# Linear attention and MoE kernel: chunks handled in pairs, two tokens per partition

## The chip, the cores and the metric

The kernel runs on one core of a Trainium2 chip. The metric is the device time of one execution in microseconds; the time of the kernel before is the median of the runs shown. TensorE (PE) multiplies matrices, VectorE (DVE), ScalarE (ACT) and GpSimd (POOL) work element by element, SyncE (SP) issues DMAs.

## The reference

For 4 batches and 8 heads of 768 tokens with 48 channels, a recurrent linear attention with a decay for each channel feeds a two-layer MoE:

```python
for t in range(S):                       # S = 768, D = 48
    state = alpha[:, :, t, :, None] * state + np.einsum('bhd,bhe->bhde', k[:, :, t], v[:, :, t])
    y[:, :, t] = np.einsum('bhd,bhde->bhe', q[:, :, t], state)
x = y.transpose(0, 2, 1, 3).reshape(B * S, H * D)       # 3072 x 384
h = x @ w_in                                            # w_in 384 x 2048
r = np.maximum(h, 0.0)
g = s * (r * r) + b
return (g @ w_out).astype(np.float32)                   # w_out 2048 x 384
```

## The kernel before

The tokens are cut into 24 blocks of 128 (six per batch), one token on each partition. The recurrence is worked out by blocks. A block's logarithms of alpha (L292, ScalarE) are summed down the tokens by a matmul with a triangle of ones (L298), and four tiny matmuls give the sum over the whole block (L303). ScalarE takes exp of the sums and of their negatives (L312, L315) and of the last sums (L316). VectorE multiplies q by the first and k by the second (L325, L330). q and k are then transposed, in the first nine blocks by TensorE (L342) with a copy out of PSUM by VectorE (L365), and after those by a DMA transpose that ScalarE's queue issues (L347). A matmul makes k times v for the state (KV, L356), with v cast to bf16 on GpSimd (L319). VectorE adds the old state (L381, or L377 at the start of a batch) and GpSimd scales it by the block's decay (L392). TensorE makes the 128 by 128 scores of all heads (A, L398), VectorE masks them (L407), 28 small matmuls make y (L436), and ScalarE copies y into the MoE's input (L460).

The MoE works on groups of blocks, four groups of two blocks and four of four. Its first layer (L482) is 48 matmuls of 256 or 512 columns per group, read out by ScalarE's Relu (L491) and squared on VectorE (L499). Its second layer (L506) is 16 matmuls of 384 columns for each block, scaled and shifted by VectorE (L517) and stored from SP's queue (L529). The b part of g is carried by column sums of w_out (L264, L269) and a matmul at L279. w_in and w_out arrive in four quarters each through four staging tiles (`wst`), are cast by ScalarE (L243, L256), and are loaded between the first blocks.

PSUM holds `ct_ps` (sums, then transposes), `a_ps` (scores), `py_ps` (KV, then y), two tiles for the first layer and two for the second.

The order of all instructions is fixed ahead of time by a planner, the class `Schedule`. Each operation is recorded with an engine, a planned length, a priority, and the buffers that it reads and writes. The planner plays the engines forward and emits the instructions in the order of planned starts. The order on an engine's queue therefore doesn't change at run time; an instruction that waits holds those behind it. `want(n)` sets the due time of a block's attention, `NPE` the number of blocks transposed on TensorE, and from block `NAY` on, the scores of a block are issued in one piece with y of the block before. `LOADS` gives the order of the first loads on SP's queue. In gaps that the planner foresees before the second layer starts, `fill` issues matmuls without use (L674).

Of the kernel before, what the change touches and what calls it, by code (L numbers as in the profile page):

```python
# [21 lines left out]
NPE = 9  # L22

NAY = 13
# [5 lines left out]
LOADS = ["b0", "b1", "i0", "b2", "b3", "i1", "i2", "i3", "b4", "o0", "b5", "o1", "o2", "b6", "o3"]  # L30
# [100 lines left out]
def kernel(  # L131
# [16 lines left out]
    C = 128  # L148
    NCH = S // C
    NP = H // 2  # L150
    NBLK = B * NCH
    d_model = moe_w_in.shape[0]
    d_ff = moe_w_in.shape[1]
    NJ = d_ff // 128
    NIN = 5
# [5 lines left out]
    ct_ps = ps.tile([128, 512], FP32, name="ct_ps")  # L161
    cum_ps = ct_ps[:, 0:384].rearrange("a (h d) -> a h d", h=H)
    bl_ps = ct_ps[:, 384 : 384 + NP]
    t_ps = ct_ps.bitcast(BF16).rearrange("a (x p t) -> a x p t", x=2, p=NP)
    a_ps = ps.tile([128, 2, NP, 128], FP32, name="a_ps")
    py_ps = ps.tile([128, 512], FP32, name="py_ps")
    p_ps = py_ps[:, 0:384].rearrange("a (p e) -> a p e", p=NP)
    y_ps = py_ps[:, 0:384].rearrange("a (k t) -> a k t", k=3)
# [3 lines left out]
    def many(name, n, shape, dtype, zero=None):  # L172
        tiles = []
        for i in range(n):
            t = sb.tile(shape, dtype, name=f"{name}{i}")
            if zero is not None:
                zero.memset(t, 0.0)
            tiles.append(t)
        return tiles


    a_in = many("a_in", NIN, [128, H, D], FP32)
    q_in = many("q_in", NIN, [128, H, D], FP32)
    k_in = many("k_in", NIN, [128, H, D], FP32)
    v_in = many("v_in", NIN, [128, H, D], FP32)
# [3 lines left out]
    def load(n, src, dst):  # L189
        b, c = n // NCH, n % NCH  # L190
        nc.sync.dma_start(  # L191
            out=dst[n % NIN],
            in_=src[b, :, c * C : (c + 1) * C, :].rearrange("h s d -> s h d"),
# [4 lines left out]
    nc.scalar.preload_act_table_set("natural_log_exp_and_others")  # L198

    la_sb = many("la", 2, [128, H, 64], BF16, zero=nc.vector)  # L200
    U_bf = sb.tile([128, 128], BF16, name="U_bf")
    make_upper_triangular(nc, U_bf, 1.0, diag=True)
    ident_bf = sb.tile([128, 128], BF16, name="ident_bf")
# [3 lines left out]
    ones_col_bf = sb.tile([128, 1], BF16, name="ones_col_bf")  # L207
    nc.vector.memset(ones_col_bf, 1.0)
    vp_sb = many("vp", 4, [128, NP, VW], BF16, zero=nc.gpsimd)
    mask = sb.tile([128, 128], BF16, name="mask")  # L210
    make_upper_triangular(nc, mask, 1.0, diag=True)
    b_sb = many("b_s", 2, [128, H, D], FP32)
    binv_sb = many("binv", 2, [128, H, D], FP32)
    qk_sb = many("qk", 3, [128, 2, H, 64], BF16, zero=nc.vector)
    qkT_sb = many("qkT", 3, [128, 2, NP, 128], BF16)
    am_sb = many("am", 2, [128, 2, NP, 128], BF16)
    blast_sb = many("blast", 2, [128, NP], BF16)
# [72 lines left out]

    def st_ln(n):
# [417 lines left out]
```

## Time and profile before

| what | value |
|---|---|
| median of 2 runs | 201.03 us (200.18 and 201.87) |
| span of the profiled execution, first to last instruction | 196.9 us |
| the profiled execution's own time | not given apart; the two runs lie 3.3 and 5.0 us above its span |
| busy: TensorE, VectorE, ScalarE, GpSimd | 176.7, 141.0, 109.1, 37.5 us |
| granted TensorE clock | 1.000 |
| DMA packets under 512 bytes | 116,256 of 122,936 |
| q, k, v and alpha load, one block and one tensor | 192 KB, 1,024 rows of 192 bytes |
| last quarter of w_out lands | 51.9 us |

Times in the profile count from the first instruction of the execution. Busy time of TensorE includes the matmuls without use. A line such as `L482` is the line in the kernel that issued the instruction; `SPq` and `ACTq` are the queues of those engines with the DMAs that they issue. In the chain of waits each step is followed back to what released it.

### The profile page before, as it was taken

To read this page: it belongs to the slowest core of one execution; us is meant where nothing else is said; L and a number is where in the kernel's file an instruction comes from. 1 tells how busy PE (TensorE), PEld (TensorE's weight loads), DVE (VectorE), ACT (ScalarE), POOL (GpSimd) and SP (SyncE) were. 2 spreads that over 40 slices of the span, in tenths; PEclk is the share of its full clock that TensorE was granted. 3 is DMA by queue.
4 is the path that set the end of the run, shared out by engine and by line. 5 is a ranking of instruction groups with operands and counts; after the bars stand their busy time and mean duration, and the time that the engine had idled before them with its cause. 6 is when DMAs were issued, how large, how long until landed. Compare 5 with 4: busy or idle time off the path is not lost.

```text
span 196.9 us, 4940 instructions
## 1 busy us (share of the span) xinstructions
PE 176.7 (90%) x1903; PEld 105.5 (54%) x1921; DVE 141.0 (72%) x288; ACT 109.1 (55%) x225; POOL 37.5 (19%) x63
## 2 busy tenths in 40 slices
PE   1789969658699999999999999999999999999992
PEld 1345557446365777766555555555555555555560
DVE  4357948679899879985999887897988544444221
ACT  4245588749674477555487655766764564444200
POOL 8622202200412212121213331032131000000000
PEclk9999999999999999999999999999999999999999
DMA  6999898997989999999999999999925210011122
GB/s 134 181 279 203 276 315 210 195 342 163 267 168 220 218 229 184 269 191 221 149 255 222 183 248 213 226 168 238 197 67 71 68 42 7 35 40 40 43 82 80
DMA packets 122936, 34.15 MB, mean 173 GB/s; under 512 B 116256, under 2 KB 121376, under 8 KB 122912
## 3 DMA queue, kind: packets, MB, share of 16 engines
q1 hardware_dynamic: 107008, 29.89, 68.7%
q10 hardware_dynamic: 15840, 3.93, 15.0%
q8 instruction: 15, 0.25, 0.6%
q14 instruction: 9, 0.07, 0.1%
q0 software_dynamic: 64, 0.00, 0.0%
HBM read 25.17 MB, written 4.72 MB: 152 GB/s over the span
## 4 chain that ended last, share of the span: by engine, by line
PE 65%; DMA 15%; SPq 10%; ACT 3%; DVE 3%; issue 2%; ACTq 0%; DVEq 0%
PE o_ps_69 L506 15%; PE o_ps_68 L506 14%; PE h_ps_67 L482 12%; PE h_ps_66 L482 12%; SPq L191 9%; PE py_ps L436 4%; DMA wst_183<-in_moe_w_in_dram 3%; DMA wst_182<-in_moe_w_out_dram 3%; DMA wst_181<-in_moe_w_out_dram 3%; DMA wst_184<-in_moe_w_out_dram 3%; PE a_ps L398 3%; DMA q_in_77<-in_q_dram 2%; PE ct_ps L298 1%; ACT w_out_bf L256 1%; PE py_ps L356 1%
## 5 line engine op out<-in xcount | busy, mean ns | idle before, releaser
L482 PEld LDWEIGHTS <-w_in_bf 128*128 128x128 bf16 x384 | 35.3, 98 | 22.4 <-ACT w_in_bf L243 1.0
L491 ACT ACTIVATE r_158<-h_ps_66 128x512 bf16<-128x512 f32 x48 | 28.9, 602 | 26.8 <-PE h_ps_66 L482 11.2
L491 ACT ACTIVATE r_159<-h_ps_67 128x512 bf16<-128x512 f32 x48 | 28.9, 602 | 4.6 <-PE h_ps_67 L482 1.8
L482 PE MATMUL h_ps_67<-xd_156,w_in_bf 128*128 128x512 bf16 (+1 forms) x71 | 16.2, 343 | 0.1
L482 PE MATMUL h_ps_66<-xd_156,w_in_bf 128*128 128x512 bf16 (+1 forms) x67 | 15.8, 341 | 0.3
L407 DVE TENSOR_TENSOR am_141<-a_ps,mask 128x1024 bf16<-128x1024 f32 x12 | 14.6, 1221 | 0.6 <-PE a_ps L398 0.4
L407 DVE TENSOR_TENSOR am_142<-a_ps,mask 128x1024 bf16<-128x1024 f32 x12 | 14.7, 1223 | 0.2
L482 PE MATMUL h_ps_66<-xd_155,w_in_bf 128*128 128x256 bf16 (+1 forms) x70 | 13.0, 306 | 1.1 <-ACT w_in_bf L243 0.8
L482 PE MATMUL h_ps_67<-xd_155,w_in_bf 128*128 128x256 bf16 (+1 forms) x71 | 13.0, 307 | 0.1
L674 PE MATMUL o_ps_68<-zeros,ident_bf 128*128 128x512 bf16 x41 | 12.0, 412 | 0.2
L312 ACT ACTIVATE b_s_129<-ct_ps 128x384 f32<-128x384 f32 x12 | 5.9, 492 | 8.5 <-PE ct_ps L303 6.4
L482 PE MATMUL h_ps_67<-xd_157,w_in_bf 128*128 128x256 bf16 (+1 forms) x46 | 9.6, 323 | 0.4 <-ACT r_159 L491 0.2
L312 ACT ACTIVATE b_s_128<-ct_ps 128x384 f32<-128x384 f32 x12 | 5.9, 489 | 7.1 <-PE ct_ps L303 2.4
L482 PE MATMUL h_ps_66<-xd_157,w_in_bf 128*128 128x256 bf16 (+1 forms) x45 | 9.6, 323 | 0.2
L460 ACT ACTIVATE xd_156<-py_ps 128x384 bf16<-128x384 f32 x10 | 4.9, 494 | 6.8 <-PE py_ps L436 3.5
L298 PE MATMUL ct_ps<-la_97,U_bf 128*128 128x384 bf16 x12 | 4.1, 340 | 4.2 <-POOL mask masks.py:65 4.1
L392 POOL TENSOR_TENSOR s_st_149<-t_147,blast_144 128x384 bf16<-128x384 bf16 x4 | 3.6, 906 | 15.3 <-DVE t_147 L381 7.9
L674 PEld LDWEIGHTS <-ident_bf 128*128 128x128 bf16 x45 | 4.2, 103 | 4.4 <-issue 1.6
L392 POOL TENSOR_TENSOR s_st_151<-t_145,blast_143 128x384 bf16<-128x384 bf16 x4 | 3.6, 904 | 14.5 <-DVE t_145 L381 7.1
L460 ACT ACTIVATE xd_155<-py_ps 128x384 bf16<-128x384 f32 x8 | 3.9, 493 | 3.9 <-PE py_ps L436 2.8
L315 ACT ACTIVATE binv_131<-ct_ps 128x384 f32<-128x384 f32 x12 | 5.9, 496 | 0.0
L315 ACT ACTIVATE binv_130<-ct_ps 128x384 f32<-128x384 f32 x12 | 5.9, 490 | 0.0
(263 smaller groups left out, 438.3 us busy)
## 6 DMA issues: line engine op xcount, KB each, us to landing
out_dram<-o_sb_176 SPq DMA_DIRECT2D x8, 192.0 KB, 3.0
out_dram<-o_sb_177 SPq DMA_DIRECT2D x8, 192.0 KB, 2.5
out_dram<-o_sb_178 SPq DMA_DIRECT2D x8, 192.0 KB, 2.4
a_in_70<-in_alpha_dram SPq DMA_DIRECT2D x5, 192.0 KB, 4.1
q_in_75<-in_q_dram SPq DMA_DIRECT2D x5, 192.0 KB, 5.1
k_in_80<-in_k_dram SPq DMA_DIRECT2D x5, 192.0 KB, 4.6
v_in_85<-in_v_dram SPq DMA_DIRECT2D x5, 192.0 KB, 4.0
a_in_71<-in_alpha_dram SPq DMA_DIRECT2D x5, 192.0 KB, 5.3
```

Of the source, the lines that this page charges most:

```text
L191: nc.sync.dma_start(out=dst[n % NIN], in_=src[b, :, c * C : (c + 1) * C, :].rearrange("h s d -> s h d"),)
L298: nc.tensor.matmul(out=cum_ps, lhsT=U_bf, rhs=la[:, :, 0:D], start=True, stop=True)
L312: nc.scalar.activation(out=b_sb[n % 2], in_=cum_ps, func=AF.Exp)
L315: nc.scalar.activation(out=binv_sb[n % 2], in_=cum_ps, func=AF.Exp, scale=-1.0)
L392: nc.gpsimd.tensor_tensor(out=s_sb[n % 3], in0=t1_sb[n % 2], in1=bl, op=ALU.mult)
L407: nc.vector.tensor_tensor(out=am_sb[n % 2].rearrange("a e p t -> a (e p) t"), in0=a_ps.rearrange("a e p t -> a (e p) t"), in1=mask.unsquee ...
L436: nc.tensor.matmul(out=y_ps[32 * (x % 4) : 32 * (x % 4) + 32, x // 4, :], lhsT=(st[:, p, c0 : c0 + 32] if e is None else vp[:, p, c0 + 48 ...
L460: nc.scalar.activation(out=xd_sb[g % 3][:, :, t * C : (t + 1) * C], in_=y_ps, func=AF.Copy)
L482: nc.tensor.matmul(out=hp[:, i * n : (i + 1) * n], lhsT=w_in_bf[:, kk, 128 * j : 128 * (j + 1)], rhs=xd_sb[g % 3][:, kk, 0:n], start=(kk = ...
L491: nc.scalar.activation(out=r_sb[w % 2], in_=h_ps[w % 2], func=AF.Relu)
L506: nc.tensor.matmul(out=op[:, 0:d_model], lhsT=gt_sb[j][:, c0 : c0 + C], rhs=w_out_bf[:, j, :], start=(j == 0), stop=(j == NJ - 1),)
L674: nc.tensor.matmul(out=o_ps[0], lhsT=ident_bf, rhs=zeros, start=True, stop=True)
```

## The change

Two blocks of 128 tokens become a pair. Token 2p and token 2p+1 of the pair lie on partition p (slot j = 0 and 1), so that a load reads 384 bytes in a row instead of 192; there are 48 such loads of 384 KB where there were 96 of 192 KB. The first half of the partitions (c = 0) is the first chunk of the pair, the second half the second chunk. Three pairs of input tiles take the place of five single ones.

The decay sums run over partitions, at half the resolution in tokens: alpha of both slots is multiplied (`st_aa`), and one Ln, one triangle matmul and one pair of exps serve both. The missing slot is made up by multiplying q of slot 0 by 1/alpha of slot 1 (`st_r1`, `st_qr`) and k of slot 0 by alpha of slot 1 (`st_ka`). V is needed by chunk: half the rows are cast in place on GpSimd, half are moved between the partition halves by VectorE (`st_vmove`), and a second cast copy (`vc`) serves KV. KV becomes 16 matmuls over 64 partitions for a pair. The transposes work on 16 blocks for a pair, on TensorE for the first three pairs (with copies shared by ScalarE and VectorE) and then as two DMA transposes of 64 partitions, now on SP's queue. The tokens of a chunk stay in the order (slot, partition) up to the copy of y, which puts them back in order. PSUM is divided anew: transposes share `a_ps` with the scores; the decay sums, KV and y share two tiles `x_ps`. From pair 2 on, `AHEAD` records the front of the next pair ahead of the back of this one. The loads of `s` and `b` move from GpSimd's queue to ScalarE's. The planner's lengths and the order of the first loads are set for this.

```diff
-NPE = 9
-NAY = 13
+NPE = 3
+NAY = 6
+AHEAD = 2
-LOADS = ["b0", "b1", "i0", "b2", "b3", "i1", "i2", "i3", "b4", "o0", "b5", "o1", "o2", "b6", "o3"]
+LOADS = ["p0", "i0", "i1", "p1", "i2", "i3", "o0", "o1", "p2", "o2", "o3"]
...
-    ct_ps = ps.tile([128, 512], FP32, name="ct_ps")
...
+    t_ps = a_ps.rearrange("a e p t -> a (e p t)").bitcast(BF16).rearrange(
+        "a (x b t) -> a x b t", x=2, b=2 * NP
+    )
+    x_ps = [ps.tile([128, 512], FP32, name=f"x_ps{i}") for i in range(2)]
+    cum_ps = x_ps[0][:, 0:384].rearrange("a (h d) -> a h d", h=H)
+    p_ps = [x[:, 0:384].rearrange("a (p e) -> a p e", p=NP) for x in x_ps]
+    y_ps = [x[:, 0:384].rearrange("a (k t) -> a k t", k=3) for x in x_ps]
...
     def load(n, src, dst):
-        b, c = n // NCH, n % NCH
+        b, c = n // PSEQ, n % PSEQ
         nc.sync.dma_start(
-            out=dst[n % NIN],
-            in_=src[b, :, c * C : (c + 1) * C, :].rearrange("h s d -> s h d"),
+            out=dst[n % NIN].rearrange("a h j d -> a h (j d)"),
+            in_=src[b, :, c * 2 * C : (c + 1) * 2 * C, :].rearrange(
+                "h (s j) d -> s h (j d)", j=2
+            ),
         )
...
+    nc.scalar.dma_start(out=b_col, in_=moe_b.to_broadcast((128, 1)))
+    nc.scalar.dma_start(out=s_col, in_=moe_s.to_broadcast((128, 1)))
...
+    def vector_or_gpsimd(n):
+        return nc.vector if n == 0 else nc.gpsimd
+
+    def st_aa(n):
+        a = a_in[n % NIN]
+        vector_or_gpsimd(n).tensor_tensor(
+            out=aa_sb[0], in0=a[:, :, 0, :], in1=a[:, :, 1, :], op=ALU.mult
+        )
+
     def st_ln(n):
-        nc.scalar.activation(
-            out=la_sb[n % 2][:, :, 0:D], in_=a_in[n % NIN], func=AF.Ln
-        )
+        nc.scalar.activation(out=la_sb[n % 2][:, :, 0:D], in_=aa_sb[0], func=AF.Ln)
+
+    def st_r1(n):
+        nc.scalar.activation(out=r1_sb[0], in_=a_in[n % NIN][:, :, 1, :], func=AF.Ln)
+        nc.scalar.activation(out=r1_sb[0], in_=r1_sb[0], func=AF.Exp, scale=-1.0)
+
+    def st_qr(n):
+        x = q_in[n % NIN][:, :, 0, :]
+        nc.gpsimd.tensor_tensor(out=x, in0=x, in1=r1_sb[0], op=ALU.mult)
+
+    def st_ka(n):
+        x = k_in[n % NIN][:, :, 0, :]
+        vector_or_gpsimd(n).tensor_tensor(
+            out=x, in0=x, in1=a_in[n % NIN][:, :, 1, :], op=ALU.mult
+        )
...
     def st_vcast(n):
-        nc.gpsimd.tensor_copy(
-            out=vp_sb[n % 4].rearrange("a p (x d) -> a p x d", d=D)[:, :, 0:3:2, :],
-            in_=v_in[n % NIN].rearrange("a (p e) d -> a p e d", e=2),
-        )
+        for c in range(2):
+            nc.gpsimd.tensor_copy(
+                out=v_heads(vp_of(n, c), half(c)), in_=v_slot(n, c, c)
+            )
+            nc.gpsimd.tensor_copy(
+                out=vc_sb[n % 2][half(c)].rearrange("a (p e) d -> a p e d", e=2),
+                in_=v_slot(n, c, 1 - c),
+            )
+
+    def st_vmove(n):
+        for c in range(2):
+            nc.vector.tensor_copy(
+                out=v_heads(vp_of(n, c), half(1 - c)), in_=v_slot(n, c, 1 - c)
+            )
...
-        nc.scalar.dma_start_transpose(
-            out=qkT_sb[n % 3].rearrange("a x p t -> a (x p) t"),
-            in_=qk_sb[n % 3].rearrange("a x h d -> a (x h d)"),
+    def st_Tdma(n, c):
+        nc.sync.dma_start_transpose(
+            out=qkT_sb[n % 3][:, c].rearrange("a x p (j t) -> a (x p j) t", j=2),
+            in_=qk_sb[n % 3][half(c)].rearrange("a x p j e d -> a (x p j e d)"),
         )
...
     def st_KV(n):
         for p in range(NP):
-            nc.tensor.matmul(
-                out=p_ps[:, p, :],
-                lhsT=kb[:, 128 * p : 128 * p + 128],
-                rhs=vp[:, p, 0:3:2, :],
-                start=True,
-                stop=True,
-            )
+            for j in range(2):
+                for c in range(2):
+                    v = v_heads(vp_of(n, c), half(c)) if j == c else vc[half(c)]
+                    nc.tensor.matmul(
+                        out=p_ps[c][:, p, :],
+                        lhsT=kb[half(c), p, j, :],
+                        rhs=v[:, p],
+                        start=(j == 0),
+                        stop=(j == 1),
+                    )
...
+    for n in range(NPAIR):
+        while begun < min(NPAIR, n + (2 if n >= AHEAD else 1)):
+            add_pair(begun)
+            begun += 1
+        finish_pair(n)
```

## The prediction

> **What bounds the kernel now.** I read the page first, then the chain of waits in order of time, then a table of busy time by stretch, then single lines in the timeline.
>
> ```profile
> PE 176.7 (90%) x1903; PEld 105.5 (54%) x1921; DVE 141.0 (72%) x288; ACT 109.1 (55%) x225; POOL 37.5 (19%) x63
> PE   1789969658699999999999999999999999999992
> PE 65%; DMA 15%; SPq 10%; ACT 3%; DVE 3%; issue 2%; ACTq 0%; DVEq 0%
> ...
> 46.10 5.80 DMA wst_184<-in_moe_w_out_dram
> 51.92 1.49 ACT w_out_bf L256
> 53.45 0.81 PE o_ps_68 L506 x4
> ```
>
> The chain has two parts. Up to 53.45 us it runs over SP's queue and the DMA of weights: the last quarter of w_out lands at 51.92, is cast, and the matmul that needs it starts at 53.45. From there it is TensorE almost alone, to 193.05. So the end is 53.45 plus what TensorE still has to do, and what can be won lies in the 53.45 and in TensorE's own work.
>
> ```profile
> 15.00:19.00 4.00, 3.95 (x60) 2.13 (x59) 3.31 (x6) 2.16 (x7) 1.30 (x2) 1.00 1.04 205
> 33.00:35.00 2.00, 1.95 (x24) 1.66 (x23) 0.95 (x4) 0.55 (x2) 0.20 (x1) 1.00 1.09 365
> 90.00:140.00 50.00, 49.24 (x547) 27.15 (x555) 43.29 (x82) 32.85 (x78) 11.51 (x15) 1.00 1.24 214
> 150.00:190.00 40.00, 39.84 (x278) 21.71 (x280) 18.20 (x37) 16.39 (x28) 0.00 (x0) 1.00 0.19 52
> ```
>
> Columns: stretch, length, busy PE, PEld, DVE, ACT, POOL, granted clock, DMA share, GB/s. With the 192-byte loads alone the full DMA moves 205 GB/s, with weights alone 365. From 90 to 140 TensorE is full, and VectorE has only 6.7 us of 50 free; after 150 VectorE is under half busy.
>
> **TensorE's work, counted.** Up to 53.4 us the trace has 7 decay sums (L298 and L303, 0.27 from start to the next line's start), 7 transpose sets (0.45), 7 KV (0.25), 6 A (0.33), 6 y (0.5; the first 0.33), 102 first-layer matmuls of 256 columns (0.108 each, six in 0.65) and 12 second-layer ones (0.1625, four in 0.65): 1.9+3.2+1.8+2.0+2.8+11.0+2.0 = 24.7 us. So 28.7 of the first 53.45 us are idle or filler (L674). What follows is 139.6 us without a gap; total work 164.3.
>
> **The loads.** Ahead of the last weight quarter SP issues 7 blocks (5.50 MB) now, 3 pairs (4.72 MB) after. Now: 2.5 us until data flows, 5.50/0.205 = 26.8, weights 6.29/0.365 = 17.2, together 46.5; the trace says 51.9, so 5.4 go where SP waits for staging tiles. For 384-byte packets no row exists. Bounds: 205 GB/s (twice the bytes take twice the time) and 365 (the weights' rate). A fixed part and a part by bytes, drawn through 192 bytes at 205 (15.0 ns for a packet of one engine) and 2,048 bytes at 365 (89.8 ns), gives 22.7 ns, or 270 GB/s; I take it, being nearer the 192-byte row in size. Then 2.5+17.5+17.2+5.4 = 42.6 instead of 51.9 (at 205: 48.1; at 365: 38.0).
>
> The Trainium skill, "DMA: Bandwidth & Descriptors", Specifications, speaks against a large gain: it puts line rate at 512 bytes and up, with a read-modify-write below, and 384 is below. Read strictly, 384 bytes would stay at the 192-byte row's 205 GB/s and the sum would be 5.5 us worse; that page's section "Why small descriptors are slow (HBM only)" has a fixed cost per packet instead, which is on the side of the middle value. No row here decides.
>
> **What TensorE gets done before that moment.** The cast ends 1.5 later, at 44.1. By then pairs 0 and 1 are through (per pair: sum 0.27, two transpose sets 0.9, KV 0.66, two A 0.66, two y 1.0, first pair 0.83; 6.8 in all), pair 2 has its front and one A (1.5), groups 0 and 1 their first layer (96 x 0.108 = 10.4), the two open output tiles three quarters (24 x 0.1625 = 3.9), and the bias matmul (1.3): 23.9. Idle 44.1 - 23.9 = 20.2 instead of 28.7: **8.5 off** (3.0 to 13).
>
> One new wait takes some back. From pair 2 on, the next pair's front is recorded ahead of this pair's back, and the decay sum and KV share x_ps[0]. So KV of pair 2 stands behind the sum of pair 3, whose alpha is loaded after the last weights: 42.6 + 1.5 transfer + product 0.9 + Ln 0.5 + sum 0.3 + Exp 1.2 = 47.0; y of both chunks and their copies end near 51. The second layer of groups 0 and 1 covers it (64 x 0.1625 = 10.4, less the 3.9 done: until 50.6). I charge **+1.0** for joints; with that cover gone it is 7.
>
> **TensorE's own work after.** Sums: 12 fewer x 0.27 = -3.2. Transposes: 6 blocks instead of 9, -1.4. KV: 16 matmuls of 64 rows per pair; A's eight of 64 rows take 0.33, so 0.66 instead of 2 x 0.25, +1.9 over 12 pairs (bounds: no change, or 16 x 0.0625 = 1.0 per pair and +6). Sum **-2.7** (-4.6 to +1.4). A, y and the MoE are as before.
>
> **What moves to other engines.** Per pair:
> - ScalarE: one Ln, one pair of Exps and a copy of the last sums less (0.5+0.49+0.49+0.19), a Ln and an Exp more (1.0); two transpose issues leave its queue (1.25 each). It gets freer by 3.2 us; off the path.
> - SP: gets two transposes, 18 in all where ScalarE had 15, at 1.25 to 1.95 (L347's shortest and longest row) beside four loads at 1.5 (their transfer) and two stores at 0.36: 9 to 11 of 13 us. The DMA engines spent 15.0% of the span on 15 transposes, 2.0 us each; A pair then has 5.8 of loads, 4.0 of transposes and 1 of stores: 10.8 of 13. If blocks of 64 rows cost double it is 14.8; but the share of 1.24 above shows the two kinds overlapping in the engines, so I keep 10.8 and no charge, with (14.8 - 13.0) x 9 = +16 as the far bound. A transpose that waits for q and k holds the stores and loads behind it; the loads are three pairs ahead and there are three output tiles, which hide one such wait. Not hidden, the late store stops VectorE's L517, then L506.
> - The s and b loads leave POOL (0.74 + 0.54) for ScalarE's queue, and the b product no longer stands before the first V cast (which began at 10.13): about 2 us of the first chain, given to the added product, Exp and multiplies of pair 0. Zero.
> - VectorE: two half-partition V moves. Bounds 0.25 (a 256-column square is 0.28) and 0.55 (a q product); I take 0.3 each, 0.6. The two Tcopies after the sixth block were already gone from the ninth. A pair has 4 x 0.47 + 4 x 0.36 + 2 x 1.22 for q, k, state and mask, and for its share of the MoE 8 squares at 0.34 and 2 x 0.61: 9.7, which becomes 10.3, beside 13.0 on TensorE (10.4 MoE, 2.6 attention).
> - POOL: two casts and two state products (2.8) become four casts (4 x 0.5), three products (L392's 0.85 each) and two state products: 6.3.
> - The y of an odd chunk from the eleventh on is recorded after the V cast and move of the pair two later, into the same tiles. It waits for them: 2.6 us in a loop of 13; hidden.
>
> POOL's work isn't free for VectorE:
>
> ```profile
> 95.15 1.10 POOL L392 TENSOR_TENSOR s_st_151<-t_147,blast_144 128x384 bf16<-128x384 bf16 x1 [4.54 <-DVE t_147 L381]
> 95.49 1.18 DVE L330 TENSOR_TENSOR qk_136<-k_in_84,binv_130 128x384 bf16<-128x384 f32 x1
> ...
> 49.62 2.12 POOL L319 CAST vp_119<-v_in_86 128x384 bf16<-128x384 f32 x1 [9.98 <-DMA v_in_86<-in_v_dram]
> ```
>
> A q or k product takes 0.55 alone and 1.18 beside a POOL product; a cast of 0.50 took 2.12 between VectorE products. Over the trace, 15 products and squares ran 7.8 us in all over their short form, in 30.3 us of such POOL work: 0.26. With 6.3 us per pair that is 1.6, so VectorE needs 11.9 of 13.0, and its waits get short. I charge **+1.5** for a squeeze (bounds: 0, and 15 as in rival 1).
>
> **Sum.** 196.9 - 8.5 + 1.0 - 2.7 + 1.5 = 188.2 span. The two times shown are 200.18 and 201.87, median 201.03, which is 4.1 above the span of the profiled execution; its own time is not told apart, and I keep the 4.1: **192.3 us**, -4.3%. Its own range is 185 to 199 (load rate -4.6 to +5.5, KV +4.1).
>
> **Rivals.**
> 1. VectorE becomes the bound. If each of a pair's 12 products and squares is hit for 0.63 as often as POOL is busy (6.3 of 13, or 7.8 when it is stretched: 0.48 to 0.6), the loss is 3.6 to 4.5 and a pair costs 13.9 to 14.8 against 13.0. Over the nine pairs 3 to 11 that is +8 to +16 instead of 1.5: 199 to 207, middle 203. For it: the 43.29 of 50. Against: by the same rule the trace would show 1.6 per pair now (POOL busy 0.22 of the time from 53 to 150), and it shows 0.65.
> 2. Slower: POOL becomes the chain. Pair n+1 starts with a product on POOL, behind the state product of pair n, which waits for VectorE. Attention must end 25 us before the end (last group's 20.8 and the tail), so nine pairs have 188.2 - 25 - 44.1 = 119 us, 13.2 each. Above that each us costs nine. With the 6.3 us doubled (a cast of 0.50 has been seen at 2.12) and 3 us of waiting, a pair takes 15.6: +21.6, 214 us. It is slower than before from 14.2 us on, and by 2% from 14.6. For it: the 2.12; in order, nine instructions per pair. Against: nearly all other casts took 0.50 to 0.83.
> 3. The loads don't speed up: 384 bytes at 205 GB/s, +5.5: 197.8, no change that can be told. For it: no row of such packets. Against: the weights' 365.
>
> **How the numbers follow.** The measurement tells about 2% from no change (197.0 and 205.1 are the bounds). Forecast 0.52, rival 1 0.17, rival 2 0.22, rival 3 0.09. In that order, faster: 0.50 + 0.04 + 0 + 0.04 = 0.58; same: 0.02 + 0.11 + 0.01 + 0.05 = 0.19; slower: 0 + 0.02 + 0.21 + 0 = 0.23. The range reaches from the forecast's low end, 184 with one us of free squeeze, into rival 2, 208.
>
> **What would show it.** Right: about 270 GB/s in the stretches with loads alone; the last weight landing near 42.6; the first matmul on it near 44; TensorE full from about 50; VectorE over 90% in the middle; 12 of L298's matmul. Wrong: TensorE idle in the middle slices with VectorE or POOL as the releaser, products on POOL above 1.2 us, or idle time before L506 released by SP's stores. If the last weight lands after 48, the load term failed.

## The result and the profile after

The changed kernel takes **217.7 us** (217.05 and 218.35) against 201.03 before: a ratio of 1.092, interval 1.067 to 1.117. It is slower by 9%; the forecast was 192.3 us, with a range up to 208. Ratios in this document compare undisturbed executions alone, each time with executions of the kernel before from the same session, and medians take all, so that a ratio and the quotient of two medians can differ by 0.01.

The page of the changed kernel, in the lines that answer to those of before (busy time; TensorE in 40 slices; then VectorE and the granted clock in slices; the chain by engine and by line):

```profile
span 216.6 us, 4926 instructions
PE 181.0 (84%) x1913; PEld 102.9 (48%) x1932; DVE 166.6 (77%) x310; ACT 110.9 (51%) x204; POOL 86.4 (40%) x121
PE   0789785777588976968895977999999999999993
DVE  3667599999999899999989599999959674444321
PEclk9999999999999999999998895799999999999999
PE 42%; DVE 31%; DMA 11%; SPq 8%; issue 5%; ACT 1%; DVEq 0%
PE o_ps L588 20%; PE h_ps L564 16%; DVE gt L581 10%; SPq L197 6%; DMA k_in<-in_k_dram 5%; DMA wst<-in_moe_w_out_dram 5%; DVE qk L405 5%; DVE vp L392 4%; DVE am L484 4%; DVE t L458 3%; PE x_ps L514 2%; DMA v_in<-in_v_dram 2%; PE a_ps L475 2%; DVE qk L397 2%; SPq L262 2%
```

TensorE's own work hardly grew (181.0 us against 176.7). Its idle time did: 216.6 - 181.0 = 35.6 us against 20.2, which is 15.4 of the 19.7 that the span grew by. (By medians of the times the growth is 16.7: the profiled execution of the kernel before is one of its quickest. In every run after it, time and span lie 1.7 to 2.0 us apart, so that a span of 196.9 goes with about 198.7 us.) VectorE has 25.6 us more to do, GpSimd 48.9 more, and VectorE has gone from 3% to 31% of the chain. Before, TensorE was full from slice 12 (54 us); now it is full from slice 26 (135 us).

The chain of waits of the changed kernel in order of time (start, length, what), where the kernel before had its last wait for weights and then TensorE alone:

```profile
17.75 9.90 DMA wst<-in_moe_w_out_dram
27.68 0.97 DVE colsum L291
...
48.33 2.15 DVE gt L581 x4
...
50.73 0.85 DVE qk L397
51.58 0.47 DVE bias_w L315
52.05 1.13 DVE am L484
53.18 0.26 DVE t L458
53.47 0.36 DVE t L458
53.86 0.35 DVE vp L392
54.23 0.89 DVE vp L392
```

The chain's last wait for weights is over at 27.65. From then on to about 100 us the chain is for the most part squares, products, masks, states and the new V moves (`vp L392`), one behind another on VectorE; from 100 to 138 us it goes back and forth between TensorE and VectorE. Three waits for loads stand in it too, of k at 69.60 and 107.75 us and of v at 85.97, 13.8 us together. Two stretches of the changed kernel, and then the longer of them in the kernel before (columns as in the prediction):

```profile
90.00:140.00 50.00, 41.14 (x459) 21.45 (x463) 45.08 (x72) 25.48 (x52) 29.61 (x38) 0.90 0.90 199
53.00:138.00 85.00, 69.35 (x855) 41.26 (x861) 78.18 (x146) 41.89 (x87) 45.28 (x54) 0.94 0.81 179
```

```profile
53.00:138.00 85.00, 84.07 (x990) 51.05 (x1001) 73.86 (x151) 52.80 (x125) 18.23 (x26) 1.00 1.17 212
```

From 53 to 138 us TensorE is busy 69.35 us of 85 where it was 84.07: 14.7 us lost in one stage, with VectorE at 78.18. GpSimd works two and a half times as long there. The granted clock, 1.00 before, is 0.94 in this stage.

What the new work costs, from the groups of the changed kernel (line, engine, operation, shapes, count; busy us, mean ns of one; idle before it and what ended that):

```profile
L581 DVE TENSOR_TENSOR gt<-r 128x256 bf16<-128x256 bf16 (+1 forms) x128 | 55.2, 465 | 20.8 <-ACT r L573 20.2
L484 DVE TENSOR_TENSOR am<-a_ps,mask 128x1024 bf16<-128x1024 f32 x24 | 29.3, 1220 | 1.1 <-PE a_ps L475 0.8
L405 DVE TENSOR_TENSOR qk<-k_in,binv 128x384 bf16<-128x384 f32 x24 | 19.3, 827 | 1.6 <-DMA k_in<-in_k_dram 1.5
L392 DVE CAST vp<-v_in 64x384 bf16<-64x384 f32 x24 | 13.8, 574 | 1.0 <-DMA v_in<-in_v_dram 0.4
...
L336 POOL TENSOR_TENSOR q_in<-q_in,r 128x384 f32<-128x384 f32 x12 | 13.7, 1138 | 15.0 <-DMA q_in<-in_q_dram 10.3
L340 POOL TENSOR_TENSOR k_in<-k_in,a_in 128x384 f32<-128x384 f32 x11 | 13.3, 1206 | 6.0 <-DMA k_in<-in_k_dram 6.0
L323 POOL TENSOR_TENSOR aa<-a_in 128x384 f32<-128x384 f32 x11 | 12.1, 1102 | 3.2 <-DMA a_in<-in_alpha_dram 2.8
```

The moves take 574 ns each where the sum had 300, GpSimd's products 1.10 to 1.21 us where it had 0.85, and a k product on VectorE averages 827 ns. (The square's mean is over two widths, 64 of 256 columns and 64 of 512, in this kernel and in those below.)

### The profile page after: what moved, and what is told of

It is laid out like the page before. It is cut to its first block, busy times and chain, and to the rows that moved or that the text cites. A ratio compares the mean times of both kernels' runs of the same rounds, so it can differ in the third digit from the quotient of the medians.

```text
span 216.6 us, 4926 instructions
## 1 busy us (share of the span) xinstructions
PE 181.0 (84%) x1913; PEld 102.9 (48%) x1932; DVE 166.6 (77%) x310; ACT 110.9 (51%) x204; POOL 86.4 (40%) x121
## 4 chain that ended last, share of the span: by engine, by line
PE 42%; DVE 31%; DMA 11%; SPq 8%; issue 5%; ACT 1%; DVEq 0%
PE o_ps L588 20%; PE h_ps L564 16%; DVE gt L581 10%; SPq L197 6%; DMA k_in<-in_k_dram 5%; DMA wst<-in_moe_w_out_dram 5%; DVE qk L405 5%; DVE vp L392 4%; DVE am L484 4%; DVE t L458 3%; PE x_ps L514 2%; DMA v_in<-in_v_dram 2%; PE a_ps L475 2%; DVE qk L397 2%; SPq L262 2%
## 5 line engine op out<-in xcount | busy, mean ns | idle before, releaser
L573 ACT ACTIVATE r<-h_ps 128x512 bf16<-128x512 f32 x96 | 56.4, 599 | 61.7 <-PE h_ps L564 25.9
L564 PE MATMUL h_ps<-xd,w_in_bf 128*128 128x256 bf16 (+1 forms) x368 | 75.4, 328 | 8.9 <-ACT r L573 7.4
L588 PE MATMUL o_ps<-w_out_bf,gt 128*128 128x384 bf16 x384 | 75.9, 330 | 7.1 <-DVE gt L581 4.3
L581 DVE TENSOR_TENSOR gt<-r 128x256 bf16<-128x256 bf16 (+1 forms) x128 | 55.2, 465 | 20.8 <-ACT r L573 20.2
L588 PEld LDWEIGHTS <-gt 128*128 128x128 bf16 x384 | 36.4, 98 | 37.4 <-DVE gt L581 7.6
L564 PEld LDWEIGHTS <-w_in_bf 128*128 128x128 bf16 x384 | 35.6, 98 | 31.9 <-issue 11.8
L468 POOL TENSOR_TENSOR s_st<-t,blast 128x384 bf16<-128x384 bf16 x16 | 16.1, 1008 | 55.8 <-DVE t L458 49.9
L484 DVE TENSOR_TENSOR am<-a_ps,mask 128x1024 bf16<-128x1024 f32 x24 | 29.3, 1220 | 1.1 <-PE a_ps L475 0.8
L599 DVE SCALAR_TENSOR_TENSOR o_sb<-o_ps,s_col,bias_w 128x384 f32<-128x384 f32 x24 | 14.8, 616 | 12.6 <-PE o_ps L588 12.4
L405 DVE TENSOR_TENSOR qk<-k_in,binv 128x384 bf16<-128x384 f32 x24 | 19.3, 827 | 1.6 <-DMA k_in<-in_k_dram 1.5
L538 ACT ACTIVATE xd<-x_ps 128x384 bf16<-128x384 f32 x24 | 14.4, 601 | 10.3 <-PE x_ps L514 10.1
L336 POOL TENSOR_TENSOR q_in<-q_in,r 128x384 f32<-128x384 f32 x12 | 13.7, 1138 | 15.0 <-DMA q_in<-in_q_dram 10.3
L397 DVE TENSOR_TENSOR qk<-q_in,b_s 128x384 bf16<-128x384 f32 x24 | 14.3, 632 | 0.5 <-ACT b_s L360 0.4
L385 POOL CAST vc<-v_in 64x384 bf16<-64x384 f32 x24 | 14.6, 607 | 0.0
L392 DVE CAST vp<-v_in 64x384 bf16<-64x384 f32 x24 | 13.8, 574 | 1.0 <-DMA v_in<-in_v_dram 0.4
```

What stands on the lines that cost most here:

```text
L385: nc.gpsimd.tensor_copy(out=vc_sb[n % 2][half(c)].rearrange("a (p e) d -> a p e d", e=2), in_=v_slot(n, c, 1 - c),)
L392: nc.vector.tensor_copy(out=v_heads(vp_of(n, c), half(1 - c)), in_=v_slot(n, c, 1 - c))
L397: nc.vector.tensor_tensor(out=qk_sb[n % 3][:, 0, :, j, :, 0:D], in0=q_in[n % NIN][:, :, j, :].rearrange("a (p e) d -> a p e d", e=2), in1= ...
L405: nc.vector.tensor_tensor(out=qk_sb[n % 3][:, 1, :, j, :, 0:D], in0=k_in[n % NIN][:, :, j, :].rearrange("a (p e) d -> a p e d", e=2), in1= ...
L468: nc.gpsimd.tensor_tensor(out=s_sb[m % 3], in0=t1_sb[m % 2], in1=bl, op=ALU.mult)
L484: nc.vector.tensor_tensor(out=am_sb[m % 2].rearrange("a e p t -> a (e p) t"), in0=a_ps.rearrange("a e p t -> a (e p) t"), in1=mask.unsquee ...
```

## The experiments

The theories: **V**, VectorE became the bound, by its V moves and by GpSimd's products, which slow it down; **Q**, the transposes on SP's queue hold up loads and stores; **P**, GpSimd's queue is itself the chain; **S**, the structure of pairs (later, larger steps) costs the time whoever does the work.

### One part of the change taken away at a time

The V moves left out:

```diff
     def st_vmove(n):
-        for c in range(2):
-            nc.vector.tensor_copy(
-                out=v_heads(vp_of(n, c), half(1 - c)), in_=v_slot(n, c, 1 - c)
-            )
+        pass
```

> The changed kernel without VectorE's V moves between the partition halves; every other instruction keeps its place, and the rows of V that are not moved stay zero. Theory V (VectorE is the bound until about 137 us, by the moves and by what GpSimd's work costs it): the moves are 13.8 us of VectorE's busy time, so 217.7 falls by 12 to 15, to 203 to 206. Theory Q (SP's queue, with the transposes ahead of the loads, is the bound): 215 to 219. Theory P (GpSimd's chain of casts and products is the bound): 214 to 218.

Measured: 209.75 us, ratio 1.048 (1.038 to 1.058). VectorE 156.7 us, GpSimd 87.9. The moves are worth 8 to 9 us. All three theories missed: the time fell, which Q and P didn't give, but by less than V gave, since VectorE lost only 9.9 of the 13.8 us of the moves (its k products, for one, got longer: 863 ns).

The three products on GpSimd left out (`st_aa`, `st_qr`, `st_ka`, each `pass`; the Ln reads slot 0):

```diff
-        nc.gpsimd.tensor_tensor(out=x, in0=x, in1=r1_sb[0], op=ALU.mult)
+        pass
```

> The changed kernel without the three products per pair on GpSimd (and the two of pair 0 on VectorE): the logarithm is taken of slot 0 alone, and q and k of slot 0 stay unscaled. All else keeps its place. Theory V: GpSimd's busy time falls from 86 to about 50, and with it a third of a us of VectorE's time for each us: 217.7 falls by 11 to 15, to 203 to 207, and the mean of VectorE's k product falls from 0.83 towards 0.6. Theory P: at least as much, 195 to 205, but with VectorE's instructions no shorter. Theory Q: 214 to 218.

Measured: 202.59 us, ratio 1.013 (1.003 to 1.024). The products are worth 15 to 16 us of time, though all but two of them run on GpSimd. The time is just below V's range and inside P's; what tells the two apart is the length of VectorE's instructions, which P had unchanged. The groups of this kernel:

```profile
L574 DVE TENSOR_TENSOR gt<-r 128x256 bf16<-128x256 bf16 (+1 forms) x128 | 48.2, 409 | 19.0 <-ACT r L566 18.3
L477 DVE TENSOR_TENSOR am<-a_ps,mask 128x1024 bf16<-128x1024 f32 x24 | 29.3, 1219 | 1.1 <-PE a_ps L468 0.8
L398 DVE TENSOR_TENSOR qk<-k_in,binv 128x384 bf16<-128x384 f32 x24 | 14.9, 645 | 1.6 <-DMA k_in<-in_k_dram 1.5
L385 DVE CAST vp<-v_in 64x384 bf16<-64x384 f32 x24 | 11.9, 496 | 1.1 <-DMA v_in<-in_v_dram 0.6
```

The same instructions on the same data shapes: the square falls from 465 to 409 ns, the k product from 827 to 645, the move from 574 to 496. The mask, which reads PSUM, stays at 1220 and 1219. VectorE loses 16.5 us for 38.0 us less on GpSimd; 1.1 of it are two products of the first pair that VectorE itself did, so (16.5 - 1.1)/38.0 = 0.41 us of VectorE for each us of GpSimd.

The Trainium skill, "GPSIMD Engine Reference", 1. Specifications, says that GpSimd shares its SBUF interfaces with VectorE and that there is contention with VectorE's instructions that have two SBUF inputs or run in a 2-port performance mode. The rows of the square and the k product, with both inputs in SBUF, agree, and so does the unchanged mask, with one input in PSUM. The move has a single SBUF input and gets shorter all the same; in which mode it ran, no run here shows. The page gives no size.

Both left out:

> The changed kernel without the V moves and without the three products (both parts of the computation left out as in the two runs above). Theory V: VectorE is no longer the bound and TensorE is, as in the kernel before; with weights that land by about 40 us the time is 186 to 194, below the kernel before. Theory P: the same within 3 us of the run without products. Theory Q: 212 to 217.

Measured: 197.99 us, ratio 0.989 (0.982 to 0.997). VectorE 137.5 us, GpSimd 49.4. V holds in direction: the two parts together are worth 20 us. Q's 212 to 217 is far off, with the transposes still on SP's queue. V missed in size, since the time stays above the 186 to 194 that it gave; what remains is taken up below. Against the kernel without moves, the products' 38.5 us of GpSimd cost VectorE (156.7 - 137.5 - 1.1)/38.5 = 0.47 us each.

The transposes on another queue:

```diff
-        nc.sync.dma_start_transpose(
+        nc.scalar.dma_start_transpose(
```

> The changed kernel with the DMA transposes issued from ScalarE's queue again, as before the change; planned there as the kernel before plans them. Theory Q: loads no longer stand behind transposes on SP's queue, the three waits of about 5 us for k and v in the chain go: 203 to 208. Theory V: VectorE's work is the same, and ScalarE's readouts come a little later: 216 to 220.

Measured: 220.1 us, ratio 1.097 (1.085 to 1.110), VectorE 166.6 us as in the changed kernel. No gain, where Q gave 203 to 208. ScalarE's queue is not free either, as a later run shows, so this run alone doesn't prove SP's queue harmless; that the loss goes away in the kernel with neither part, whose transposes stay on SP, says more.

### The suspected cost put into the kernel before

If V is right, the same work in the kernel before, with nothing of the pairs, must slow it down. Two products on GpSimd behind each V cast; one copy across partition halves on VectorE in each block; both:

```diff
+        for _ in range(2):
+            nc.gpsimd.tensor_tensor(out=xo_sb, in0=x_sb[0], in1=x_sb[1], op=ALU.mult)
...
+        nc.vector.tensor_copy(out=xv_sb[0:64], in_=x_sb[0][64:128])
```

> The kernel before the change with GpSimd work added and nothing else: behind each V cast, two 128x384 products in fp32 on scratch tiles whose result nobody reads (48 in all, some 50 us). No pairs, no moves, the old loads and queues. Theory V (VectorE loses 0.41 to 0.47 us for each us of GpSimd work, as the runs with and without products give it): VectorE's busy time rises from 141 to about 161 and the time from 201.4 to 206 to 212. Rival S (the structure of the pairs, with its queues and longer chains, costs the time, and GpSimd's work is hidden): 200 to 203.

> The kernel before the change with one copy of 64 partitions x 384 from fp32 to bf16, from the upper to the lower partitions, added on VectorE in front of each k product (24 in all, on scratch tiles). Theory V: VectorE has 13% free from 60 to 140 us, and 24 x 0.4 = 10 us go mostly into it: 202 to 206. Rival S: 200 to 203.

> The kernel before the change with both additions of the two runs above. Theory V: VectorE's busy time is about 172, above that of the changed kernel (166.6), without its quicker loads: 213 to 224. Rival S: 200 to 205.

Measured: products alone 210.8 us, ratio 1.056 (1.053 to 1.059); copies alone 205.07, ratio 1.028 (1.024 to 1.032); both 224.0, ratio 1.112 (1.101 to 1.122). All three are inside what V gave, and none is where S had it. The added work has no reader, so nobody waits for its results, and the loss is that of busy engines alone. Both together cost more than the two singly (11.2% against 5.6% and 2.8%), as one would expect once VectorE has no room left. Structure S is not needed for a loss of this size. Nor is P: in the kernel with products alone no engine waits for GpSimd longer than 2.2 us in all, once for a V cast, and the kernel before waited so too (2.3 us). A line of the page, two groups and a stretch of the kernel with products alone:

```profile
PE 184.1 (88%) x1921; PEld 107.5 (51%) x1921; DVE 160.4 (77%) x288; ACT 108.4 (52%) x225; POOL 91.5 (44%) x113
...
L504 DVE TENSOR_TENSOR gt<-r 128x256 bf16<-128x256 bf16 (+1 forms) x128 | 58.9, 487 | 17.8 <-ACT r L496 17.1
L412 DVE TENSOR_TENSOR am<-a_ps,mask 128x1024 bf16<-128x1024 f32 x24 | 29.3, 1219 | 0.8 <-PE a_ps L403 0.4
...
53.00:138.00 85.00, 78.70 (x921) 47.71 (x921) 78.83 (x144) 47.76 (x111) 46.20 (x49) 1.00 1.02 192
```

VectorE has not one instruction more than before (288) and is busy 160.4 us instead of 141.0, for 54.0 us more on GpSimd: 0.36. Again the mask stays at 1219. From 53 to 138 us TensorE is busy 5.4 us less than in the kernel before (84.07), at a granted clock of 1.00 in both, so that this loss isn't the clock's.

### The loads alone undone

```diff
+        for j in range(2):
             nc.sync.dma_start(
-                out=dst[n % NIN].rearrange("a h j d -> a h (j d)"),
+                out=dst[n % NIN][:, :, j, :],
```

> The changed kernel with each load split by slot into two of 192-byte rows, as the kernel before has them; the layout and all else stay. If the loads' rate falls back to about 205 GB/s, the weights land some 9 us later (41 now at the cast, then 50). Theory V: VectorE is the bound from 30 us on, but its early work waits for the same loads, so a part of the 9 us comes through: 219 to 225. If nothing of the quicker loads reaches the end: 217 to 219.

Measured: 226.29 us, ratio 1.132 (1.126 to 1.138), four points above the changed kernel: the 384-byte loads are worth some 8 us. That is a little more than V gave (219 to 225). The last quarter of w_out lands at 48.5 us instead of 39.4. The edit also doubles the loads that SP issues, so the 8 us are for both. The stretch from 20 to 50 us, first with the split loads, then in the changed kernel:

```profile
20.00:50.00 30.00, 20.73 (x246) 12.98 (x244) 22.37 (x40) 19.07 (x29) 11.86 (x16) 0.94 0.96 252
```

```profile
20.00:50.00 30.00, 22.79 (x276) 14.04 (x273) 27.41 (x47) 21.97 (x36) 16.07 (x18) 1.00 1.05 315
```

With slow loads VectorE, the later bound, gets through 5 us less of its work there, and that work is missing later.

### Ways to keep the pairs without the cost

The V moves as a DMA between the halves of SBUF, from the bf16 copy, on SP's queue (V in three sets, `vc` laid out like `vp`):

```diff
-            nc.vector.tensor_copy(
-                out=v_heads(vp_of(n, c), half(1 - c)), in_=v_slot(n, c, 1 - c)
-            )
+            nc.sync.dma_start(
+                out=vp_of(n, c)[half(1 - c)], in_=vc_sb[n % 2][half(c)]
+            )
```

> The changed kernel with the V moves taken from VectorE: each half goes from the bf16 copy to the other partitions by a DMA on SP's queue (two per pair, 64 rows of 1152 bytes), with V in three sets of tiles and one set for the inverse decays instead of two. All of the computation is there. If VectorE is the bound (theory V): VectorE loses 13.8 us, as in the kernel without the moves, and the time comes to that kernel's, 208 to 212 us, with VectorE busy 152 to 158 us. If what that kernel gained came from having nobody wait for the moves (rival S, the structure of the pairs): the DMA lands two to four microseconds after the cast where the copy took 0.6, and the time stays at 215 us or above.

Measured: 212.22 us, ratio 1.053 (1.046 to 1.060), VectorE 157.1 us. At the upper edge of what V gave (208 to 212), and level with the kernel without any moves, although the moved rows now land 2.8 us after the issue. Rival S (215 or above), for this part, falls.

To this, the sums of both slots by TensorE instead of products on GpSimd:

```diff
+        for j in range(2):
+            for x, u in ((0, V_bf), (1, U_bf)):
+                nc.tensor.matmul(out=cums_ps[x], lhsT=u if j else U_bf,
+                    rhs=la[:, j, :, 0:D], start=(j == 0), stop=(j == 1))
```

> The kernel before this one, and the half-resolution sums undone inside the pairs: the logarithms of both slots are summed by TensorE (four matmuls of 384 columns instead of one, and eight short ones instead of four per pair) and exponentiated for both slots, so that GpSimd's three products per pair and ScalarE's reciprocal go, and the decays have one set of tiles each. All of the computation is there. Theory V: VectorE as in the kernel with neither moves nor products, 136 to 142 us busy, GpSimd 48 to 51 us; the time that kernel's 198.0 us plus up to 4 us for TensorE's added sums (about 0.7 us per pair, partly in its gaps): 198 to 203 us. Rival S: the time stays above 205 us although VectorE is as free as there.

Measured: 209.52 us, ratio 1.042 (1.037 to 1.048). VectorE 141.0 and GpSimd 49.8 us, both as V expected; the time wasn't, and it lies where rival S had it (above 205). The page and the sum's groups show another reason than S:

```profile
PE 186.7 (90%) x2014; PEld 108.8 (52%) x2033; DVE 141.0 (68%) x284; ACT 112.6 (54%) x204; POOL 49.8 (24%) x94
...
L334 PE MATMUL x_ps<-la,U_bf 128*128 128x384 bf16 x36 | 10.3, 341 | 6.6 <-ACT la L324 6.6
L344 PE MATMUL x_ps<-half_bf,la 128*128 128x2 bf16 x96 | 4.2, 164 | 0.0
L334 PE MATMUL x_ps<-la,V_bf 128*128 128x384 bf16 x12 | 4.1, 343 | 0.0
```

TensorE idles 207.5 - 186.7 = 20.8 us, as in the kernel with neither (195.5 - 174.2 = 21.3), but is busy 12.5 us more. The sums take 10.3 + 4.2 + 4.1 = 18.6 us where the kernel with neither has 4.1 + 2.9 = 7.0. So here TensorE itself is the bound, and its added work counts in full (the time is 11.5 us above that kernel's); I had hidden part of it in gaps. The kernel with three sums, further down, tests this.

The V casts on ScalarE besides, and the same in the kernel before:

```diff
-            nc.gpsimd.tensor_copy(
-                out=v_heads(vp_of(n, c), half(c)), in_=v_slot(n, c, c)
+            nc.scalar.activation(
+                out=v_heads(vp_of(n, c), half(c)), in_=v_slot(n, c, c), func=AF.Copy
             )
```

> The kernel before this one with the V casts on ScalarE instead of GpSimd, which keeps only the states. Theory V: GpSimd's 28 us of casts go, and at 0.4 to 0.5 us of VectorE per us of GpSimd VectorE falls by some 10 us more, to 124 to 132 us busy; TensorE fills from earlier, and the time is 192 to 198 us, under the kernel before the change. Rival A: ScalarE takes 48 casts more at 0.45 us, about 22 us on its 111, and the relu that feeds the squares comes late; the time is then at or above 199 us although VectorE is under 132 us.

> The kernel before the change with its V cast on ScalarE instead of GpSimd: 24 casts fewer there, nothing of the pairs. Theory V: VectorE loses about 5 us of 141 busy, but TensorE has no more gaps to close after 53 us in the kernel before, so the time falls by 0 to 2 us, 198 to 201 us. If GpSimd's load matters apart from VectorE (rival P): 196 us or less.

Measured: 212.23 us, ratio 1.057 (1.050 to 1.064), and 205.19 us, ratio 1.011 (1.001 to 1.021). Both missed V's ranges, and P's 196 or less falls. The first is slower than the kernel that it changes (1.057 against 1.042), the second no faster: GpSimd down to 21.7 and VectorE to 133.4 us (in the pairs) bring nothing where VectorE isn't the bound. ScalarE has 134.2 us instead of 112.6, and TensorE's idle time rises from 20.8 to 23.5. That the relu is late by the casts, as rival A has it, fits, but no run separates it.

One matmul of four saved, with one product back on GpSimd, and that kernel with its transposes on ScalarE's queue:

```diff
-        for j in range(2):
-            for x, u in ((0, V_bf), (1, U_bf)):
...
+        for x, u, j in ((0, U_bf, 0), (0, neg_bf, 1), (1, U_bf, 0)):
```

> The whole computation: V moves by DMA, and of the products only that of the two decay slots on GpSimd, in place; TensorE sums it, and takes the odd slot's logarithm off for the even tokens with a negative identity, three matmuls of 384 columns per pair instead of four, and four short ones instead of eight. Theory T (the kernel with four sums was bound by TensorE's own work, 12.5 us more busy than the kernel with neither at the same idle time): TensorE loses 3.4 us and the time falls from 209.5 to 205 to 207 us. Theory V (VectorE is still what counts): the product on GpSimd costs VectorE 12 x 1.1 x 0.44 = 6 us, and the time stays at 209 us or above.

> The kernel before this one with its DMA transposes on ScalarE's queue instead of SP's. In the kernel with four sums TensorE was idle for some 6 us between 90 and 140 us while the chain ran through loads of the decays. Theory Q: those loads were queued behind transposes and V moves on SP's queue, the gaps close by 4 us, and the time is 200 to 203 us, level with the kernel before the change. Rival D: within 1.5 us of the kernel before this one. [...]

Measured: 205.25 us, ratio 1.025 (1.019 to 1.031), inside what T gave (205 to 207), and V's 209 or above falls: TensorE 180.4 us busy, idle 23.3. It is the fastest form of the pairs with the whole computation, and the kernel before is still ahead by 2.5%. The second took 217.61, ratio 1.084 (1.077 to 1.091), far above both theories. The kernel with neither moves nor products missed both of its theories in the same way when its transposes went to ScalarE's queue:

> The changed kernel without the V moves and without the three products (the other partitions' halves of V are zero, the decays are those of one slot), and its DMA transposes on ScalarE's queue instead of SP's. With VectorE free, TensorE still stood idle for 4.3 us between 80 and 130 us in the kernel with neither. Theory Q (with VectorE free, the loads that wait on SP's queue behind transposes are what TensorE waits for): those gaps close and 198.0 us becomes 193 to 195.5 us. Rival D (the gaps come from elsewhere: too few sets of input tiles, or the square's and mask's turn on VectorE): 197 to 199.5 us.

Measured: 205.87 us, ratio 1.027 (1.018 to 1.037), where the same kernel with SP's queue had 0.989. Its chain and the row of its transposes (18 issues; shortest, median, longest in ns):

```profile
76.06 1.51 ACTq L416
...
99.11 3.22 ACTq L416
```

```profile
L416 ACTq DMA_TRANSPOSE qkT<-qk x18: 1257/1346/3224, 53.6 to 150.4; - x18
```

An issue of 1.3 to 3.2 us stands in ScalarE's order ahead of relu and copies of y, and it is on the chain 5% of the span. The plan allowed 0.8 us for one, although the trace of before had 1.25 to 1.95 (L347). In these kernels SP is the better place, as the changed kernel has it. As a test of Q these runs fail: they take a load off one queue and put a worse one on another.

## Why the prediction was wrong, point by point

The forecast was 25.4 us too low. Of this, 18.2 are the moves and products, which cost 217.7 - 198.0 = 19.7 us where the sum had 1.5; 7.2 are missing without them too (198.0 against 192.3 - 1.5 = 190.8).

**The rate of the loads was right, the moment of the cast by luck.** The changed kernel's DMA in two stretches with 384-byte loads alone, 40 to 44 and 44 to 48 us:

```profile
DMA packets 2912, 1.11 MB, mean 277 GB/s; under 512 B 2911, under 2 KB 2911, under 8 KB 2911
```

```profile
DMA packets 3092, 1.18 MB, mean 296 GB/s; under 512 B 3091, under 2 KB 3091, under 8 KB 3091
```

277 and 296 GB/s against the 270 taken between 205 and 365. (The stretch with 365 was not of weights alone: 585 of its 989 packets were under 512 bytes, and the rows of w_out have 1,536 bytes, not 2,048. From 36 to 37 us of the changed kernel, with 244 of 248 packets larger, it is 375.) The last quarter of w_out was issued at 32.08 us and landed 7.3 us later, at 39.4, before the forecast's 42.6. Its cast began only at 44.02, since ScalarE's order had relus, the cast of the third quarter and a copy ahead of it, some of which waited for VectorE and TensorE:

```profile
wst<-in_moe_w_out_dram SPq DMA_DIRECT2D x1, 768.0 KB, 7.3
```

```profile
44.02 1.48 ACT L283 ACTIVATE w_out_bf<-wst 128x1536 bf16<-128x1536 f32 x1
```

It ended at 45.5 us (forecast 44.1; before, 53.4), and the first matmul on it began at 45.71. Two errors nearly cancel there; in the kernel with neither part the cast began at 40.15. The Trainium skill's "DMA: Bandwidth & Descriptors", Specifications, with its 512 bytes for line rate, is borne out in that 384 bytes stay under the weights' rate; but 384 bytes are already well above the 205 of 192 bytes, which is the direction of the fixed overhead per packet in that page's section "Why small descriptors are slow (HBM only)", and a read-modify-write that keeps all below 512 slow doesn't show. Rival 3 falls.

**TensorE's own work agrees in the net only.** Without the moves and products TensorE is busy 174.2 us, 2.5 less than before; the sum had 2.7 less. Busy times of single lines overlap, so the terms can't be told apart this way, and one was too large: KV was taken at 0.66 us for a pair, and its 16 matmuls stand in the chain of the changed kernel with 0.45 us (at 122.24 and 146.84).

**The step that failed is the +1.5 for VectorE's squeeze.** The prediction named every part of it and mis-sized four, all the same way; what it had at 1.5 us is worth 19.7:

| term | taken | measured |
|---|---|---|
| a V move on VectorE | 0.30 us | 0.574 (0.39 in a quiet spot, 0.439 in the kernel before) |
| a product on GpSimd | 0.85 us | 1.10 to 1.21 |
| a V cast on GpSimd | 0.50 us | 0.57 to 0.61 |
| VectorE lost for each us of GpSimd | 0.26 us | 0.41 and 0.47 (0.36 in the kernel before) |

By the prediction's own working a pair then has on GpSimd 3 x 1.15 + 4 x 0.59 + 2 x 1.0 = 7.8 us and on VectorE 9.7 + 2 x 0.574 + 7.8 x 0.44 = 14.3 us where it had 11.9, beside 13.0 on TensorE. (The 0.574 holds some of the same slowing, so this is a little high.) That is over the line that rival 1 drew, and rival 1 (13.9 to 14.8) was the mechanism, at 0.17. Its argument against itself was that the trace of before showed only 0.65 us per pair lost, the same 7.8 us as in the 0.26. That rate mixes two: in the trace of before some 6 of the 7.8 us lie beside the 14.9 us of state products (0.4), and some 2 beside the 15.3 us of casts (0.1), an estimate from the overlap of the instructions. So the row for products of two inputs was there, with about the 0.41 to 0.47 that the fp32 products then showed.

Rival 1's time, 199 to 207, was too low as well. It charged the excess over 13.0 in nine pairs to a kernel that otherwise won 8.5 us. The trace shows instead VectorE busy 103.0 of 110 us from 30 us to 140: there was little left in which it could catch up, and squares that TensorE's second layer reads come late. A part of the loss can be the granted clock: 0.66 in the stretch from 130 to 140 and 0.976 over the span, where the kernel with neither part had 0.997. It is at most (1 - 0.976) x 216.6 = 5.2 us, an estimate that charges the whole drop to the end; executions of the kernel before with a mean clock of 0.974 and 1.000 took 200.89 and 199.24 us. The two drops to 0.5 come right after stretches in which TensorE was busy about half the time (2.01 of 4.30 us up to 117.3, 1.87 of 3.50 up to 131.0), which fits a clock that falls because TensorE waits. No run separates the two.

**The +1.0 for KV of pair 2** can't be told apart: from 46 to 56 us the chain has VectorE's work and no KV. **The transposes on SP at no charge:** from 50 to 60 us the DMA moves 12 GB/s, because the loads stand behind a transpose that SP's queue holds for 11.5 us, until 58.5, for a k product of VectorE; that is VectorE's lateness passed on by SP's order, and the 13.8 us of load waits in the chain may be so too. No run gained by moving the transposes, but none tested them cleanly. **Rival 2**, GpSimd as the chain: by time it was nearest (214), but GpSimd itself waits 49.9 us for VectorE's state sums, and no engine waits for a product on GpSimd longer than 1.6 us in all.

**The second step that failed is the 8.5 off.** It was to come from idle time of TensorE, matmuls without use included, that falls from 28.7 us up to 53.4 to 20.2 us up to 44.1. The stretch up to 44 us in the changed kernel and in the kernel with neither part:

```profile
0.00:44.00 44.00, 30.39 (x339) 17.64 (x343) 32.62 (x62) 27.30 (x41) 25.35 (x46) 1.00 0.96 292
0.00:44.00 44.00, 31.26 (x359) 18.64 (x363) 29.99 (x60) 30.94 (x48) 17.74 (x38) 1.00 0.95 288
```

The matmuls without use are 12.27 and 11.30 us of these busy times, so 25.9 and 24.0 us are idle or without use. By the same reckoning the kernel before has 53.4 - 38.18 + 11.96 = 27.2 up to 53.4: 1.3 us are won by that moment, and 3.1 without moves and products, instead of 8.5. The kernel with neither part reached 198.0. Its windows:

```profile
30.00:40.00 10.00, 8.47 (x111) 6.02 (x104) 9.96 (x21) 8.47 (x16) 3.39 (x5) 1.00 0.99 306
40.00:50.00 10.00, 8.82 (x121) 5.26 (x122) 9.94 (x19) 7.81 (x16) 3.75 (x5) 1.00 0.98 253
...
90.00:100.00 10.00, 8.74 (x77) 4.27 (x79) 8.42 (x18) 5.98 (x13) 0.97 (x1) 1.00 1.17 229
...
110.00:120.00 10.00, 8.52 (x123) 4.81 (x123) 7.55 (x14) 7.03 (x16) 6.11 (x10) 1.00 1.06 258
```

VectorE is full (9.96 and 9.94 of 10) in the very stretch in which the earlier weights should have filled TensorE, which points at squares of the first groups that were not there to be multiplied. The prediction counted TensorE's work up to 44.1 us and never VectorE's. Later, from 80 to 130 us, TensorE idles 4.1 us where the kernel before idled 0.4, and the chain there runs through two loads of alpha of 5.0 and 6.0 us. Both are read from the trace and not tested; whether those loads are late by SP's order or by having three input tiles is open.

**The 4.1 from span to time** is for the most part not a cost of each execution: in all later runs it is 1.7 to 2.0. The rest is the distance of the profiled execution of before from the median, so as a step from that span to the median it stands.

## What to carry to other kernels

Work that goes to GpSimd isn't off the books of VectorE: here each us of GpSimd's fp32 products cost VectorE 0.36 to 0.47 us in most kernels, in instructions whose inputs lie in SBUF, and nothing that shows in the mask, which reads PSUM. Where a change brings the bound of a stage forward in time, count in that stage the work of every engine that feeds it, not of the bound alone. And a row priced in a quiet spot, or a contention rate averaged over other instructions, was too low here for a place that the change made busy.

## What the runs showed of the hardware beyond this

- Beside GpSimd's products a chain of squares is held up visibly; in the timeline of the changed kernel (start, length):

```profile
115.92 3.22 DVE L581 TENSOR_TENSOR gt<-r 128x512 bf16<-128x512 bf16 x4
...
116.33 1.04 POOL L323 TENSOR_TENSOR aa<-a_in 128x384 f32<-128x384 f32 x1
117.34 1.18 POOL L336 TENSOR_TENSOR q_in<-q_in,r 128x384 f32<-128x384 f32 x1
```

  Four squares of 512 columns take 3.22 us, 0.81 each, where the mean of that width is 0.532 in the changed kernel and 0.450 in the one with neither part.
- Not all of GpSimd's work slows VectorE alike. Taking its V casts away freed 7.6 us of VectorE for 28.1 us of GpSimd (0.27) in the pairs, and 2.6 for 15.3 (0.17) in the kernel before; fp32 products of two inputs cost 0.36 to 0.47. Nor is that rate fixed: in the kernel with three sums 8.3 us more of GpSimd's time, eleven such products, left VectorE only 1.3 us busier than with four sums (142.3 against 141.0), 0.6 of it a product of its own, where theory V had 6. Presumably it depends on what VectorE does beside the product; that was not measured.
- A DMA transpose is issued for 1.3 to 3.2 us of the issuing engine's order, so its cost depends on whose queue it stands in: moved to ScalarE's, with the plan changed to match, it cost the kernel with neither part 3.8 points of its ratio.
